# How four stores of a decode-attention backward kernel are cut, and on which queue one row leaves

## The chip, the core and the metric

The kernel runs on one core of one Trainium2 chip. The core has a matrix engine (PE, TensorE), three engines for elementwise work (DVE is VectorE, ACT is ScalarE, POOL is GpSimd), an engine that here only issues transfers (SP, SyncE), and 16 DMA engines that move data between the chip's memory (HBM) and the core's on-chip memory (SBUF). The metric is the device time of one execution in microseconds (us), as a median over runs. The profile is of one execution of its own; its "span" begins and ends inside that execution.

## The reference

Forward attention of a single query row per head over 8192 keys, with 32 heads of width 128 in bfloat16, and its gradients for a given output gradient:

```python
def _fwd_reference(q, k, v):
    scale = q.shape[-1] ** -0.5
    scores = jnp.einsum('bhqd,bhkd->bhqk', q, k) * scale
    attn = _softmax(scores, axis=-1)
    return jnp.einsum('bhqk,bhkd->bhqd', attn, v)

def reference(q, k, v, grad_out):
    ...
    _out, _vjp = jax.vjp(_f, q, k, v)
    _grads = _vjp(grad_out)
    ...
    return (_out0, *[jnp.asarray(_g) for _g in _grads])
```

The inputs are q (1, 32, 1, 128), k and v (1, 32, 8192, 128) and grad_out like q. The kernel is asked for four results: the output O and dQ, which are 32 rows of 128 numbers each (8 KB), and dK and dV, which are as large as k and v (67 MB each). With p the softmax row and ds its gradient, dV is the outer product of p and the head's grad_out row, and dK is the outer product of ds and the head's q row.

## The kernel before, in words

**Tiling.** Two heads make a pair, so there are 16 pairs (`HP`), numbered 0 to 15. The K of a pair is one SBUF tile `Kt` of 128 partitions with 32 KB each, 4 MB (the profile counts it as 4096 KB), and its V is a tile `Vt` of the same size. The tiles are reused in place: when a pair's K has been read for the scores and for dQ, `outer(j, "dk", r)` (L286 to L305) overwrites it with dK, and the tile is stored from there; `Vt` becomes dV in the same way. `outer` does one eighth of a tile at a time (`r` from 0 to 7, one VectorE multiplication at L290 each). There are three K tiles (`K_BUFS`) and two V tiles (`V_BUFS`), so a load into a tile has to wait until the gradient of the pair that used it before has been stored: V of pair 3 goes into the tile from which dV of pair 1 leaves, and K of pair 5 into the tile from which dK of pair 2 leaves.

**Loop.** `for j in range(HP + 1)` (L355) does the softmax part of pair j and the gradient part of pair j-1 (`p_`). For j from 3 to 15, dK of pair j-1 is multiplied out in the middle of the step (r = 0 and 1 at L419 and L420, 2 at L433, 3 at L448, 4 to 7 at L467), then `load_v(j + 1)` is issued; then dV of pair j is multiplied out (L487) and `load_k(j + 2)` issued (L492). For j = 1 and 2 and for the last step, j = 16, the eight dK blocks come in one run (L402 to L407).

**Order.** The order of the instructions on each engine is written out by hand (`tc.manual_schedule()`, L126). All loads and stores of K, V, dK and dV go out on SyncE's queue in the order of the code, except half of dV of pair 0, which GpSimd issues in shares (`share_out`, L116). A transfer that SyncE issues first waits for what it depends on, and everything behind it on SyncE waits too.

**How a store is cut.** `outer` looks up `ENDS` (L18) for its tile: the numbers in it are the block counts after which a piece is stored. `(8,)`, which is what a tile without an entry gets, is one store of 4 MB after the eighth block; `(4, 8)` is two stores of 2 MB, after the fourth and the eighth; `(2, 4, 8)` is 1 MB, 1 MB and 2 MB. The store is issued at L305.

**The end.** In step 16 there is no new pair. dK of pair 15 is multiplied out in eight blocks, and between blocks 5 and 6 (L403) the code puts in `result` (L334 to L341) twice: it turns the collected O and dQ columns into rows through a copy on ACT, a transpose on PE and a second copy on ACT into `fin_sb`, and stores the 32 rows. The third argument says which engine's queue issues that store.

Of the kernel before, what the change touches and what calls it, by code (L numbers as in the profile page):

```python
# [14 lines left out]

XK_BUFS = 3
EARLY = 3
ENDS = {("dv", 1): (4, 8), ("dk", 2): (4, 8), ("dk", 15): (2, 4, 8), ("dv", 15): (4, 8)}  # L18
CH = 16
TB = 4  # L20
R = 4
# [10 lines left out]
def kernel(  # L32
# [11 lines left out]
    nc = tc.nc  # L44
# [44 lines left out]
    def load_v(j):  # L89
        Vt[j] = vpool.tile([P, NT, D], BF16, tag="V", name="Vt")  # L90
        parts = LOADS.get(("v", j), 1)
        for c in range(parts):
            nc.sync.dma_start(slots(Vt[j], c, parts), rows_of(v, j, c, parts))
# [74 lines left out]
    o_all = consts.tile([P, H], F32)  # L168
    dq_all = consts.tile([P, H], F32)
# [99 lines left out]
    def gather_copy(j, which):  # L269
        if j % GP != GP - 1:  # L270
            return
        S = acc["S" + which] = small.tile([P, 4, D], F32, tag="S", name="S_" + which)
        nc.scalar.copy(S[:].rearrange("p j d -> p (j d)"), acc.pop(which)[:])

    def gather(j, which, bank):
        if j % GP != GP - 1:
            return
        S, to = acc.pop("S" + which), (o_all if which == "p" else dq_all)
        pick = lane[:].rearrange("p (w j) -> p j w", j=4)
        at = 8 if which == "p" else 16  # L280
        for i in range(4):
            nc.tensor.matmul(bank[:, at:at + 2 * GP], lhsT=S[:, i, :], rhs=pick[:, i, :],  # L282
                             start=(i == 0), stop=(i == 3), skip_group_check=True)
        nc.scalar.copy(to[:, 2 * (j - GP + 1):2 * j + 2], bank[:, at:at + 2 * GP])

    def outer(j, which, r):  # L286
        x = st[j]
        G, dst = (Kt[j], out_2) if which == "dk" else (Vt[j], out_3)
        rep, row = x["ds"] if which == "dk" else x["p"], qd[j][:, 0 if which == "dk" else 1, :]
        nc.vector.tensor_tensor(  # L290
            slots(G, r, NU).rearrange("p n (a b) -> p n a b", b=R),
            slots(rep, r, NU).unsqueeze(2).to_broadcast([P, CH, D // R, R]),
            row.rearrange("p (a b) -> p a b", b=R).unsqueeze(1).to_broadcast([P, CH, D // R, R]),
            op=ALU.mult)
        if (which, j) == ("dv", 0):
            if (r + 1) * CH == SHARED:
                share_out(rows_of(dst, 0)[:, 0:SHARED, :], G[:, 0:SHARED, :])
            elif r == NU - 1:
                nc.sync.dma_start(rows_of(dst, 0)[:, SHARED:NT, :], G[:, SHARED:NT, :])
            return  # L300
        ends = ENDS.get((which, j), (8,))
        if r + 1 in ends:
            i = ends.index(r + 1)
            a, b = (ends[i - 1] if i else 0) * CH, (r + 1) * CH
            nc.sync.dma_start(rows_of(dst, j)[:, a:b, :], G[:, a:b, :])  # L305
# [25 lines left out]
        nc.vector.tensor_copy(x["ds"][:], ds1[:].unsqueeze(2).to_broadcast([P, NT, R]))  # L331
        window(ds1[:].rearrange("p (g j) -> p g j", j=4))

    def result(src, dst, issuer):  # L334
        half = small.tile([P, H], BF16, tag="half", name="half", bufs=2)
        nc.scalar.copy(half[:], src[:])
        fin_ps = psT.tile([P, 2 * TB, P], BF16, tag="T", name="fin_ps")
        nc.tensor.transpose(fin_ps[0:H, 0, :], half[:], ident[:])
        fin_sb = small.tile([H, D], BF16, tag="fin", name="fin_sb", bufs=2)
        nc.scalar.copy(fin_sb[:], fin_ps[0:H, 0, :])  # L340
        issuer.dma_start(dst.rearrange("b h s d -> (b h s) d"), fin_sb[:])  # L341

    DQ = NG // 4
    NC = NX // TB
# [5 lines left out]
    def half(j, f):  # L350
        for c in range(f * NC, (f + 1) * NC):
            chunk(j, c)
        v_scores(j, f)

    for j in range(HP + 1):  # L355
# [42 lines left out]
        if ends and j > 0:  # L398
            gather_copy(p_, "ds")
            if early:  # L400
                half(j, 0)
            for r in range(NU):  # L402
                if j == HP and r == NU - 2:  # L403
                    result(o_all, out_0, nc.scalar)
                    gather(p_, "ds", st[p_]["m"])
                    result(dq_all, out_1, nc.sync)
                outer(p_, "dk", r)  # L407
            if j + 1 < HP:
                load_v(j + 1)
# [115 lines left out]
```

## Time and profile before

| what | value |
|---|---|
| median of 3 runs | 633.3 us (633.1 to 633.46) |
| the profiled execution's own time | 633.27 us |
| its span | 631.5 us |
| busy in the span: PE, DVE, ACT, POOL | 462.9, 516.2, 205.2, 10.0 us |
| moved by DMA | 268.98 MB, 426 GB/s on average |
| read from and written to HBM | 134.23 MB each |

The profile's page cuts the span into 40 slices of 15.8 us and gives for each the share of time in which the 16 DMA engines were busy, and the rate. The timeline lists the instructions of one engine in order: start, duration, and what it is; "x2" merges two that follow each other. A line with SPq is the moment at which SyncE hands a transfer over, not the transfer. "To landing" is the time from there to the transfer's completion.

### The profile page before, as it was taken

The numbers are of one execution on the slowest core, as the hardware profiler recorded it, in microseconds if no ns is written. First come the engines' busy times: TensorE is split into PE (matmuls) and PEld (weight loads), VectorE is DVE, ScalarE is ACT, GpSimd is POOL, SyncE is SP. The second block draws the span as 40 slices with busy tenths as digits, with TensorE's granted clock in tenths as the row PEclk, the third lists the DMA queues.
The fourth block names the chain that finished last, engine by engine and source line by source line (L and its number), as shares of the span: only waits on it lengthen the run. The fifth ranks groups of instructions, "written<-read, shape, count | busy, mean of one in ns | idle before, by whom it ended". The sixth has DMA issues, their size and how long they took to land.

```text
span 631.5 us, 8017 instructions
## 1 busy us (share of the span) xinstructions
PE 462.9 (73%) x3256; PEld 247.0 (39%) x3256; DVE 516.2 (82%) x654; ACT 205.2 (32%) x460; POOL 10.0 (2%) x21
## 2 busy tenths in 40 slices
PE   4786687778787888676897767957679776796670
PEld 1443354254443525333363432624336243252440
DVE  6589887989889798796978969879597896988873
ACT  2441434053342505234151330603316143160430
POOL 2030000000000000000000000000000000000000
PEclk9989968878698977779877788877897878887785
DMA  8999999999999999999999999999999999999997
GB/s 366 432 400 436 431 435 431 429 422 439 433 431 434 431 431 438 429 432 431 429 432 433 427 432 431 431 432 427 429 436 433 432 431 431 432 431 431 428 420 323
DMA packets 12052, 268.98 MB, mean 426 GB/s; under 512 B 1904, under 2 KB 1904, under 8 KB 1904
## 3 DMA queue, kind: packets, MB, share of 16 engines
q1 hardware_dynamic: 11136, 266.35, 98.4%
q0 software_dynamic: 736, 2.10, 0.8%
q8 instruction: 25, 0.41, 0.2%
q14 instruction: 11, 0.09, 0.0%
q10 hardware_dynamic: 144, 0.02, 0.0%
HBM read 134.23 MB, written 134.23 MB: 425 GB/s over the span
## 4 chain that ended last, share of the span: by engine, by line
DMA 60%; PE 26%; DVE 8%; ACT 3%; issue 1%; DVEq 0%; SPq 0%; ACTq 0%
DMA Vt<-in_v_dram 40%; DMA out_dram<-Vt 19%; PE T_ps L215 15%; PE s_ps L198 4%; PE acc_p L265 4%; DVE Vt L290 2%; ACT XV_sb L220 2%; PE dp_ps L232 2%; DVE Kt L290 2%; DVE XK_sb L188 1%; PE acc_ds L265 1%; DMA Kt<-in_k_dram 1%; DVE sT L205 0%; PE m_ps L282 0%; DVE dpT L243 0%
## 5 line engine op out<-in xcount | busy, mean ns | idle before, releaser
L198 PE MATMUL s_ps<-XK_sb,q_win 128*128 128x512 bf16 x512 | 154.8, 440 | 63.8 <-DVE XK_sb L188 59.1
L290 DVE TENSOR_TENSOR Vt<-p_rep,qd 128x2048 bf16<-128x2048 bf16 x128 | 154.1, 1222 | 40.4 <-PE acc_p L265 30.7
L188 DVE STREAM_TRANSPOSE XK_sb<-Kt 128x1024 f32<-128x1024 f32 x128 | 150.2, 1218 | 37.8 <-DMA Kt<-in_k_dram 34.3
L215 PE MATMUL T_ps<-ident_f,Vt 128*128 128x128 f32 x1024 | 167.5, 317 | 7.0 <-DMA Vt<-in_v_dram 7.0
L220 ACT COPY XV_sb<-T_ps 128x512 f32<-128x512 f32 x256 | 140.0, 589 | 85.6 <-PE T_ps L215 85.1
L290 DVE TENSOR_TENSOR Kt<-ds_rep,qd 128x2048 bf16<-128x2048 bf16 x128 | 149.5, 1214 | 3.1 <-PE acc_ds L265 2.7
L215 PEld LDWEIGHTS T_ps<-ident_f,Vt 128*128 128x128 f32 x1024 | 133.9, 163 | 44.6 <-issue 21.7
L198 PEld LDWEIGHTS <-q_win 128*128 128x128 bf16 x512 | 52.2, 111 | 153.8 <-issue 123.1
L265 PE MATMUL acc_p<-Vt,win 128*32 128x512 bf16 x512 | 55.5, 435 | 3.6 <-ACT win L255 3.6
L440 ACT ACTIVATE e<-sT,nbias 128x128 f32<-128x128 f32 x16 | 8.3, 516 | 147.8 <-DVE nbias L436 147.8
L265 PEld LDWEIGHTS <-win 128*32 128x32 bf16 x1024 | 22.9, 99 | 60.3 <-issue 48.7
L265 PE MATMUL acc_ds<-Kt,win 128*32 128x512 bf16 x512 | 42.5, 427 | 4.6 <-ACT win L255 4.6
L255 ACT COPY win<-ds 64x128 bf16<-64x128 bf16 x32 | 9.5, 296 | 106.5 <-DVE ds L327 106.3
L232 PE MATMUL dp_ps<-XV_sb,do_win 128*32 128x512 bf16 x512 | 34.0, 381 | 13.5 <-ACT XV_sb L220 13.5
L232 PEld LDWEIGHTS <-do_win 128*32 128x32 bf16 x512 | 14.3, 94 | 29.0 <-issue 22.5
L441 PE MATMUL m_ps<-rs,ones_f 128*128 128x1 f32 x32 | 7.5, 305 | 24.4 <-ACT e L440 24.4
L427 PE MATMUL m_ps<-ident_f,top 128*128 128x128 f32 x16 | 4.8, 300 | 23.5 <-DVE top L425 23.5
L205 DVE STREAM_TRANSPOSE sT<-s_ps 128x512 f32<-128x512 f32 x16 | 11.5, 717 | 10.8 <-PE s_ps L198 10.8
L441 PEld LDWEIGHTS m_ps<-rs,ones_f 128*128 128x128 f32 x32 | 6.2, 241 | 27.6 <-ACT e L440 27.6
L452 ACT ACTIVATE p_rep<-e,rinv 128x512 bf16<-128x512 f32 x16 | 11.5, 721 | 13.3 <-DVE rinv L450 13.3
L427 PEld LDWEIGHTS m_ps<-ident_f,top 128*128 128x128 f32 x16 | 2.1, 133 | 31.0 <-issue 25.4
L317 PEld LDWEIGHTS m_ps<-pd,ones_f 128*128 128x128 f32 x32 | 8.8, 286 | 10.1 <-DVE prod L248 9.1
(59 smaller groups left out, 151.5 us busy)
## 6 DMA issues: line engine op xcount, KB each, us to landing
Kt<-in_k_dram SPq DMA_DIRECT2D x14, 4096.0 KB, 29.0
out_dram<-Kt SPq DMA_DIRECT2D x14, 4096.0 KB, 25.0
Vt<-in_v_dram SPq DMA_DIRECT2D x14, 4096.0 KB, 29.0
out_dram<-Vt SPq DMA_DIRECT2D x13, 4096.0 KB, 32.2
out_dram<-Vt SPq DMA_DIRECT2D x5, 2048.0 KB, 17.9
out_dram<-Kt SPq DMA_DIRECT2D x3, 2048.0 KB, 17.8
Kt<-in_k_dram SPq DMA_DIRECT2D x4, 1024.0 KB, 8.0
Vt<-in_v_dram SPq DMA_DIRECT2D x2, 2048.0 KB, 17.4
```

The lines of the kernel that those rows point to most:

```text
L188: nc.vector.transpose(XK[j, u][:].rearrange("p g w i -> p (g w i)"), slots(Kt[j], u, NU).rearrange("p g d -> p (g d)").bitcast(F32))
L198: nc.tensor.matmul(st[j]["s"][:], lhsT=q_win[:, c, at:at + P], rhs=cols[:, c // 2, c % 2], start=(u == 0 and c == 0), stop=(u == NU - 1 an ...
L205: nc.vector.transpose(sT[:].rearrange("p g r -> p (g r)"), x["s"][:])
L215: nc.tensor.transpose(T_ps[:, i, :], words[:, m * P:(m + 1) * P], ident_f[:])
L220: nc.scalar.copy(XV[j][:, b * TB:(b + 1) * TB, :], st[j].pop(("T", c))[:])
L232: nc.tensor.matmul(out[b * QD:(b + 1) * QD, :], lhsT=do_win[:, b // 2, e2, at:at + QD], rhs=cols[:, z, e2, :, b * QD:(b + 1) * QD], start= ...
L255: nc.scalar.copy(win[t * M:(t + 1) * M, :, at:at + 4], src[t * M:(t + 1) * M])
L265: nc.tensor.matmul(acc[which][b * QD:(b + 1) * QD, :], lhsT=win[:, g, at:at + QD], rhs=X[:, 4 * g:4 * g + 4, :].rearrange("p n d -> p (n d)"),
L290: nc.vector.tensor_tensor(slots(G, r, NU).rearrange("p n (a b) -> p n a b", b=R), slots(rep, r, NU).unsqueeze(2).to_broadcast([P, CH, D // ...
L317: nc.tensor.matmul(x["m"][:, 1:3], lhsT=ones_f[:], rhs=x["pd"][:], start=True, stop=True, skip_group_check=True)
L441: nc.tensor.matmul(x["m"][:, 0:1], lhsT=ones_f[:], rhs=rs[:], start=True, stop=True, skip_group_check=True)
L452: nc.scalar.activation(x["p"][:], e[:].unsqueeze(2).to_broadcast([P, NT, R]), ACT.Copy, scale=rinv[:])
```

## The change

Four edits, in two places. dV of pair 1 and dK of pair 2 lose their entries in `ENDS`, so each is stored as one transfer of 4 MB after its eighth block. The last 2 MB of dK of pair 15 are stored as two transfers of 1 MB, after the sixth and the eighth block. `result` loses its third argument: O's rows are issued on SyncE's queue, as dQ's were, and no longer on ACT's.

```diff
-ENDS = {("dv", 1): (4, 8), ("dk", 2): (4, 8), ("dk", 15): (2, 4, 8), ("dv", 15): (4, 8)}
+ENDS = {("dk", 15): (2, 4, 6, 8), ("dv", 15): (4, 8)}
...
-    def result(src, dst, issuer):
+    def result(src, dst):
...
-        issuer.dma_start(dst.rearrange("b h s d -> (b h s) d"), fin_sb[:])
+        nc.sync.dma_start(dst.rearrange("b h s d -> (b h s) d"), fin_sb[:])
...
                 if j == HP and r == NU - 2:
-                    result(o_all, out_0, nc.scalar)
+                    result(o_all, out_0)
                     gather(p_, "ds", st[p_]["m"])
-                    result(dq_all, out_1, nc.sync)
+                    result(dq_all, out_1)
                 outer(p_, "dk", r)
```

The built program has the same instructions in the same order on PE, DVE and POOL; ACT has one fewer (the issue of O's store). On SyncE the pair of half stores becomes one store in two places, and the end reads: dK 15 first quarter, second, third, O's rows, dQ's rows, fourth quarter.

## The prediction

> **What bounds the kernel now.** I read first the page's slices, then its DMA queues.
>
> ```profile
> DMA  8999999999999999999999999999999999999997
> GB/s 366 432 400 436 431 435 431 429 422 439 433 431 434 431 431 438 429 432 431 429 432 433 427 432 431 431 432 427 429 436 433 432 431 431 432 431 431 428 420 323
> ...
> q1 hardware_dynamic: 11136, 266.35, 98.4%
> q8 instruction: 25, 0.41, 0.2%
> ```
>
> The DMA engines are full from the second slice to the last but one; DVE, the busiest compute engine, is at 82%. q1, SyncE's queue, fills 98.4% of the engines' time. So the question of each edit is whether a DMA engine gets more or less to do, or runs dry. The windows answer the second part (the last two columns are the DMA share and GB/s; a share can pass 1, as a packet is counted where it starts):
>
> ```profile
> 60.00:72.00 12.00, 7.78 (x76) 4.74 (x78) 10.57 (x15) 6.76 (x15) 0.00 (x0) 1.00 1.03 443
> 72.00:77.00 5.00, 3.54 (x28) 1.31 (x20) 4.97 (x7) 0.41 (x2) 0.00 (x0) 1.00 1.00 426
> ...
> 129.00:136.00 7.00, 6.57 (x33) 4.82 (x34) 6.86 (x9) 4.06 (x9) 0.00 (x0) 0.55 0.99 426
> ...
> 150.00:600.00 450.00, 341.86 (x2356) 181.18 (x2359) 376.08 (x470) 146.30 (x323) 0.00 (x0) 0.83 1.00 431
> ...
> 620.00:622.00 2.00, 0.00 (x0) 0.00 (x0) 0.65 (x1) 0.00 (x0) 0.00 (x0) 0.50 1.01 419
> 622.00:625.00 3.00, 0.00 (x0) 0.00 (x0) 0.00 (x0) 0.00 (x0) 0.00 (x0) 0.50 1.08 455
> 625.00:628.00 3.00, 0.00 (x0) 0.00 (x0) 0.00 (x0) 0.00 (x0) 0.00 (x0) 0.50 0.80 344
> 628.00:631.40 3.40, 0.00 (x0) 0.00 (x0) 0.00 (x0) 0.00 (x0) 0.00 (x0) 0.50 0.08 34
> ```
>
> The share is about 1 where the edits lie, and falls only from 625 us on, when one engine after the other has finished. For more I took the trace's records of single packets. They don't say on which engine a packet ran, but a packet begins about 4 ns before the recorded end of the one ahead of it, so they can be strung into 16 chains (an inference, which worked out for all 11,136 packets of q1). Three things come out. No chain idles more than 0.6 us in the whole span. A transfer puts 8 packets and a semaphore write on each engine, and takes there, start to start, 9.681 us with 4 MB, 4.863 with 2 MB, 2.453 with 1 MB. And the chains end apart: the first at 626.46, the last four at 628.98, 629.02, 629.57 and 629.82; the span ends 1.7 us after the last. So the end is the load of the fullest DMA engine.
>
> **The change part by part.** What SyncE issues, in its timeline:
>
> ```profile
> 65.15 0.34 SPq L93 DMA_DIRECT2D Vt<-in_v_dram  x1
> 71.66 4.87 SPq L305 DMA_DIRECT2D out_dram<-Vt  x2
> 76.62 0.53 SPq L87 DMA_DIRECT2D Kt<-in_k_dram  x1
> ...
> 113.81 0.34 SPq L87 DMA_DIRECT2D Kt<-in_k_dram  x1
> 129.59 5.46 SPq L305 DMA_DIRECT2D out_dram<-Kt  x2
> 135.15 0.38 SPq L93 DMA_DIRECT2D Vt<-in_v_dram  x1
> ...
> 613.87 2.60 SPq L305 DMA_DIRECT2D out_dram<-Kt  x2
> 618.73 0.34 SPq L341 DMA_DIRECT2D out_dram<-fin_sb  x1
> 620.68 0.34 SPq L305 DMA_DIRECT2D out_dram<-Kt  x1
> ```
>
> *dV 1 whole.* The line at 71.66 holds both halves; the second starts at 71.66 + 4.87 - 0.33 = 76.20. Now all 4 MB leave then, the first half 4.5 us later. Ahead of it in the queue is V 2, issued at 65.15 and landed 19.5 us later (DMA issues), at 84.7: 8.5 us of cover. By chain, V 2 ends between 77.27 and 84.22; a store's first packet came 0.85 us after its issue at the end (620.68, 621.53), so the whole store can begin at 77.05, 0.2 us before the first engine is free. K 3 follows at 76.6 in both kernels, V 3 waits for dV 1 to land, 17.9 us after 76.20, as the second half does now. Nothing behind it moves. Gain: two pieces cost 2 x 4.863 = 9.725 us of each engine, one 9.681: -0.044. With the cover gone the cost is up to 4.5.
>
> *dK 2 whole.* The same. The second half starts at 129.59 + 5.46 - 0.33 = 134.72, 5.1 us after the first. K 4, issued at 113.81, lands 29.0 later at 142.8: 8.1 us of cover; the first chain is through at 136.27, 0.7 us after the store can begin (135.57). -0.044; cover gone, up to 5.1.
>
> *dK 15 in four.* DVE's eight multiplications run from 611.48 for 9.17 us, so the sixth ends at 611.48 + 6/8 x 9.17 = 618.36, and the third quarter leaves there; the fourth at 620.68 as the 2 MB do now. Would the earlier issue let the end come earlier? The second quarter is issued at 613.87 + 2.60 - 0.33 = 616.14 and takes 9.0 to land, until 625.1, so at 620.68 the fullest engine still has 4 us queued: by chain its first packet of the last store is at 624.95. Starting earlier helps engines that are waiting; the only ones that did, for 0.57 and 0.07 us, end at 626.51 and 626.46, over 3 us before the last. Gain 0; cost of one more boundary 2 x 2.453 - 4.863 = +0.043.
>
> *O's rows on SyncE.* ACT loses an issue of 0.33 us at 616.96, in a stretch where its next copy (L284) waits for PE until 617.62: nothing. The rows put two packets of 256 B and a semaphore write on an engine, 0.034 us, on either queue. On SyncE they stand behind the third quarter and ahead of dQ's rows and the last quarter. `fin_sb` of O is ready at 616.93, dQ's at 618.71, so three issues in a row end by 618.36 + 0.33 + 2 x 0.34 = 619.4, or 0.34 after dQ's are ready, 619.1; the last multiplication ends at 620.65. The cover is 1.3 us; without it the fourth quarter leaves later, and that counts on the fullest engine only past 627.4 (624.95 + 2.45). Bounds: 0 and +0.03.
>
> *Semaphores.* A transfer also waits for the one eight places before it, whose semaphore it reuses. In the changed program's waits the fourth quarter inherits dK 14's. That store is issued at 594.56 and lands 16.2 later at 610.8, ten before. In the stretches between, the predecessor is two pairs back. 0.
>
> **Sum**: -0.044 - 0.044 + 0.043 = -0.05 us. The profiled execution has a span of 631.5 and a time of 633.27, so 1.77 lie around it: 631.45 + 1.77 = 633.2. The median, 633.3, is 0.03 above the profiled run. 0.2% of it, 1.27 us, is about what a measurement of this kernel can tell from no change.
>
> **Rivals.** *A, slower: the fullest engine gets more.* Besides the queue's transfers the engines carry instruction fetches (the q8 row: 25 packets of 16 KB; by their records 0.95 us each, 0.87 to 1.07), spread unevenly, and slow packets (median 1.21 us for 32 KB, the longest 1.97). The changed program has one instruction fewer on ACT, and other places for three on SyncE; if that moves a fetch onto the engine that ends last, it costs 0.95 us: 634.2. One stays within 0.2%; from two on (635.1) it is past it. The other way it pays little, since the next engine ends only 0.25 us earlier. Against: PE and DVE, which have most of the instructions, keep every one; the three times before lie within 0.36 us. 17%: 10 for one, 7 for more.
>
> *B, slower: the rings run dry before the whole stores.* For it: the first chain is within 0.2 us of that at 77. Against: only the fullest matters, and it has V 2 until 84.22 and K 4 until 142.36. It decides when the whole store begins after that, some 7 us later than worked out; then it costs up to 4.5 and 5.1, for one of them 637.8. 4%.
>
> *C, faster: the last store is the end.* The span closes with SyncE waiting 9.1 us for the last dK store. If that transfer's size set the end, halving it would give 4.86 - 2.45 = 2.4 us: 630.8; if only the idle seen in front of it counted, 0.57: 632.7. Against: the share of 1.01 and 1.08 from 620 to 625, and the first packets at 624.95. 7%, five of them past 0.2%.
>
> *D, faster: a transfer has a fixed cost that queued work doesn't hide.* One transfer fewer in all. The dearest row for one is the 8 KB of q rows at the start, 3.4 us to landing (DMA issues): 629.8. Against: the steps of 2.45, 4.86 and 9.68 us, nearly in proportion to size. 4%. The Trainium skill, "DMA: Bandwidth & Descriptors", section "Anatomy of one DMA", gives a fixed part of about 2.0 us per transfer beside its bytes, measured on GpSimd's path; by that, exposed, the sum would be -2.0 and the time 631.2. The chains here show 0.043 to 0.044 us for a boundary on SyncE's queue: the rule describes a transfer by itself, and no run here has one in the places edited. The same page, "Rules for kernel authors", wants at least 1 MiB per transfer, and the new quarters are just that; paying 2.0 us at the very end would make 635.2, but the two quarters stored now follow each other without a gap.
>
> **Numbers.** The forecast, no change, has 68%, with a range of its own of 632.7 to 633.8. It holds the band of 0.2% (632.0 to 634.6) but for 1% below and 2% above. Faster: C 5 + D 4 + 1 = 10%. Slower: A 7 + B 4 + 2 = 13%. The rest, 77%, is the same. The range runs from 632.1 to 634.4: it takes in one fetch of A and C's smaller price, and leaves out C's larger (4 or 5), D (4), A's second fetch (7) and B (4), some 19%.
>
> **What will show it.** In the profile after: a DMA share of 0.97 to 1.03 around 77 and 136; dV 1 landing near 94 and dK 2 near 152.5; the third quarter issued near 618.4, O and dQ within 1.3 us behind it, the fourth at 620.7; DMA falling off from 625 and the last packet near 629.8. A share well under 1 around 77 or 136 would speak for B, an end whose slow engine holds one more 16 KB fetch for A, an end more than 1 us earlier for C or D. I am wrong if the fullest engine is not what ends the span.

## The result: 0.19% slower

| | before | changed |
|---|---|---|
| median | 633.1 us (21 runs, 632.46 to 634.49) | 634.35 us (21 runs, 633.26 to 636.27) |
| ratio | | 1.0019, 95% interval 1.0013 to 1.0026 |
| profiled execution, its span | 633.27, 631.5 | 635.82, 634.0 |

The change costs 1.2 us. One run of a version below, the profiled one of the even kernel with whole stores, took 1251.68 us at a granted clock of 0.349 and is in none of the numbers. The changed kernel's shortest run is 0.8 us above the shortest before, its longest 1.8 us above the longest, so the runs also lie further apart. The profiled execution of the changed kernel is one of the longer ones, which makes it useful. Its page first, the slices and the queues:

```profile
DMA  8999999999999999999999999999999999999996
GB/s 366 431 406 435 431 426 431 429 435 431 429 429 430 429 433 435 429 432 427 431 432 433 432 427 431 431 434 429 429 435 427 436 431 432 434 432 429 426 419 267
...
q1 hardware_dynamic: 11040, 266.36, 98.1%
q8 instruction: 25, 0.41, 0.2%
```

The DMA engines together are as full as before in every slice but the last, 267 GB/s where it was 323, and there are as many instruction fetches, 25. The windows of the end say how that slice empties (last columns: granted clock, DMA share, GB/s). First the changed kernel:

```profile
620.00:622.00 2.00, 0.36 (x2) 0.10 (x1) 1.43 (x2) 0.64 (x3) 0.00 (x0) 0.50 1.03 434
622.00:625.00 3.00, 0.00 (x0) 0.00 (x0) 0.00 (x0) 0.00 (x0) 0.00 (x0) 0.50 1.01 420
625.00:628.00 3.00, 0.00 (x0) 0.00 (x0) 0.00 (x0) 0.00 (x0) 0.00 (x0) 0.50 0.90 375
628.00:630.00 2.00, 0.00 (x0) 0.00 (x0) 0.00 (x0) 0.00 (x0) 0.00 (x0) 0.50 0.22 94
630.00:632.00 2.00, 0.00 (x0) 0.00 (x0) 0.00 (x0) 0.00 (x0) 0.00 (x0) 0.50 0.06 25
632.00:634.00 2.00, 0.00 (x0) 0.00 (x0) 0.00 (x0) 0.00 (x0) 0.00 (x0) 0.50 0.02 8
```

and the same stretches of the kernel before:

```profile
628.00:630.00 2.00, 0.00 (x0) 0.00 (x0) 0.00 (x0) 0.00 (x0) 0.00 (x0) 0.50 0.14 57
630.00:632.00 2.00, 0.00 (x0) 0.00 (x0) 0.00 (x0) 0.00 (x0) 0.00 (x0) 0.50 0.00 0
```

A share of 0.06 is one engine of 16. In the changed kernel fifteen engines are done by 630 and a single one works on alone, to 632.7; before, nothing moved after 629.8. So the average load didn't grow; one engine fell behind. The question is which one, and where. SyncE's timeline of the changed kernel:

```profile
39.07 0.35 SPq L299 DMA_DIRECT2D out_dram<-Vt  x1
...
65.31 0.34 SPq L93 DMA_DIRECT2D Vt<-in_v_dram  x1
78.17 0.33 SPq L305 DMA_DIRECT2D out_dram<-Vt  x1
78.59 0.38 SPq L87 DMA_DIRECT2D Kt<-in_k_dram  x1
...
113.97 0.34 SPq L87 DMA_DIRECT2D Kt<-in_k_dram  x1
137.18 0.33 SPq L305 DMA_DIRECT2D out_dram<-Kt  x1
...
614.65 4.87 SPq L305 DMA_DIRECT2D out_dram<-Kt  x3
619.57 2.50 SPq L341 DMA_DIRECT2D out_dram<-fin_sb  x2
622.16 1.16 SPq L305 DMA_DIRECT2D out_dram<-Kt  x1
```

dV 1 leaves at 78.17, 2.0 us later than the 76.20 that I had from the execution before, and dK 2 at 137.18, 2.5 us later than 134.72. Most of the 2 us has nothing to do with the change: the first line, dV 0's second half, which comes before any edited instruction, is at 39.07 here and was at 37.27. The compute that leads up to these stores took about 2 us more in this execution than in the other.

Strung into chains as in the prediction (a chain is one DMA engine's packets, inferred from their times), the packets of the two profiled executions give this (us; "slow chain" is explained below):

```
                                                    before            changed
V 2 ends on the slow chain, the first of the 16     77.27             77.45
dV 1 (second half / whole) issued                   76.20             78.17
the slow chain idle before dV 1                     0                 1.56
V 2 ends on the last of the 16                      84.22             84.54
slow packets on the slow chain, whole span          7.2               8.9
the slow chain ends                                 628.5             632.70
the last of the other chains ends                   629.82            629.95
```

One chain is unlike the others. Nearly every 32 KB packet takes 1.213 us. On this chain, and apart from short bursts on this one alone, many take a little longer (up to 0.13 us each), which adds up to 1.0 to 1.8 us in every 100 us of both traces from 100 us on. (Two chains can be mistaken for each other after packets of theirs end within some ns, so late in the span the identity is followed by this excess. The sums of 7.2 and 8.9 are therefore estimates, the second above all.) In the changed trace the chain that ends at 632.70 shows the excess until 622 us, so the last engine is the slow one. It is also the chain that carries next to nothing of GpSimd's queue: 0.4 us, the others 2.8 to 7.6. That is what `SHARES` does with dV 0: it leaves one engine out. In the kernel before, this engine thus starts some 4.6 us ahead at 77 us, gives that up over 500 us, and ends in the middle of the field. In the changed kernel it sits idle with its queue empty until the first packet of the whole dV 1 comes at 79.01, 0.84 us after the issue, and the head start it lost there is missing at the end.

### The profile page after: what moved, and what is told of

It is laid out like the page before. It is cut to its first block, busy times and chain, and to the rows that moved or that the text cites. A ratio compares the mean times of both kernels' runs of the same rounds, so it can differ in the third digit from the quotient of the medians.

```text
span 634.0 us, 8014 instructions
## 1 busy us (share of the span) xinstructions
PE 466.7 (74%) x3256; PEld 246.8 (39%) x3256; DVE 516.0 (81%) x654; ACT 204.1 (32%) x460; POOL 10.0 (2%) x21
## 4 chain that ended last, share of the span: by engine, by line
DMA 50%; PE 27%; DVE 16%; ACT 3%; issue 2%; DVEq 0%; ACTq 0%; SPq 0%
DMA Vt<-in_v_dram 23%; PE T_ps L215 11%; DMA Kt<-in_k_dram 10%; DMA out_dram<-Vt 9%; DMA out_dram<-Kt 8%; PE s_ps L198 7%; DVE Kt L290 6%; DVE XK_sb L188 4%; PE acc_p L265 3%; DVE Vt L290 2%; ACT XV_sb L220 2%; PE acc_ds L265 2%; PE dp_ps L232 2%; DVE sT L205 1%; PE m_ps L282 1%
## 5 line engine op out<-in xcount | busy, mean ns | idle before, releaser
L198 PE MATMUL s_ps<-XK_sb,q_win 128*128 128x512 bf16 x512 | 156.4, 442 | 66.4 <-DVE XK_sb L188 61.2
L215 PE MATMUL T_ps<-ident_f,Vt 128*128 128x128 f32 x1024 | 165.0, 313 | 5.4 <-DMA Vt<-in_v_dram 5.4
L215 PEld LDWEIGHTS T_ps<-ident_f,Vt 128*128 128x128 f32 x1024 | 130.9, 160 | 43.2 <-issue 20.5
L265 PE MATMUL acc_p<-Vt,win 128*32 128x512 bf16 x512 | 57.0, 449 | 2.9 <-ACT win L255 2.9
L184 ACT COPY do_win<-do_cols 64x4 bf16<-64x4 bf16 x32 | 6.6, 206 | 16.1 <-PE dp_ps L232 15.9
```

The costliest lines, as they stand in the source:

```text
L198: nc.tensor.matmul(st[j]["s"][:], lhsT=q_win[:, c, at:at + P], rhs=cols[:, c // 2, c % 2], start=(u == 0 and c == 0), stop=(u == NU - 1 an ...
L215: nc.tensor.transpose(T_ps[:, i, :], words[:, m * P:(m + 1) * P], ident_f[:])
L265: nc.tensor.matmul(acc[which][b * QD:(b + 1) * QD, :], lhsT=win[:, g, at:at + QD], rhs=X[:, 4 * g:4 * g + 4, :].rearrange("p n d -> p (n d)"),
```

## The experiments

The theory ("the head start"): dV 1 and dK 2, stored whole, come so late that the slow DMA engine, first through V 2 and K 4, runs dry. The rivals: the new order at the end; whole stores costing something in themselves; VectorE's work. All ratios are to the kernel before on the same chip, with a 95% interval. A ratio is not the quotient of the two medians, and differs from it by up to 0.1% (638.47 / 633.39 is 1.0080, the ratio there 1.0071).

**One edit alone, and all but it.**

```diff
 # dV 1 whole alone, on the kernel before
-ENDS = {("dv", 1): (4, 8), ("dk", 2): (4, 8), ("dk", 15): (2, 4, 8), ("dv", 15): (4, 8)}
+ENDS = {("dk", 2): (4, 8), ("dk", 15): (2, 4, 8), ("dv", 15): (4, 8)}
 # all but dV 1, on the changed kernel
-ENDS = {("dk", 15): (2, 4, 6, 8), ("dv", 15): (4, 8)}
+ENDS = {("dv", 1): (4, 8), ("dk", 15): (2, 4, 6, 8), ("dv", 15): (4, 8)}
```

> The kernel before with one of the four edits: dV of pair 1 stored whole. Theory (the head start): one of the 16 DMA engines moves its packets slower than the others all through the span and gets almost nothing of pair 0's shares, so it is the first to finish V 2, at 77.3 to 77.5 us. The whole store of dV 1 comes at 76.2 to 78.2, depending on the execution, and that engine runs dry for up to some 3 us, which it cannot make up; it ends last. Expected: the whole loss of the change, 634.3 (ratio 1.0015 to 1.0025), and an idle stretch on one chain near 77. Rival (the end): the order of the last five issues on SyncE is what costs; then 633.1, ratio 1.000. Rival (dK 2): 633.1 too.

> The changed kernel with dV of pair 1 back in two halves; the other three edits stay. The head start: 633.1, ratio 0.9995 to 1.0005, no chain idle over 0.6 us near 77. The rivals (the end, or dK 2): the loss stays, 634.3, ratio 1.0015 to 1.0025.

dV 1 whole alone: 634.09 against 633.39, ratio 1.0015 (1.0005 to 1.0025); 632.96 to 636.24 over 12 runs. As expected in size; but the profiled execution was a short one (dV 1 out at 75.94, no idle stretch, 633.39), so this trace doesn't show the loss. All but dV 1: 634.38, ratio 1.0020 (1.0009 to 1.0031). This was a miss: I had put the whole loss on dV 1, and the other three edits cost as much by themselves. The two don't add to 0.35%, as independent costs would. What the runs of the second kernel do show is a strong tie to the clock that TensorE was granted: 636.7 at 0.827, 633.02 at 0.852, correlation -0.93 over 11 runs. For the changed kernel it is -0.70 (21 runs), for the kernel before on that chip 0.05 (29 runs). It is no rule, though: for dV 1 whole alone it is -0.12 (12 runs, the longest, 636.24, at 0.843), and for the kernel before on the chip of the last experiments -0.43 (27 runs). So I widened the theory to dK 2: both are the same mechanism, and a head start can be lost only once. In the changed trace, where it went at 77 us, dK 2 could begin at 137.18 + 0.84 = 138.02 and the slow chain had K 4 until 139.37.

The trace of that second kernel does not bear the theory out. Its profiled run, 634.38 like its median, issued dK 2 at 134.58, so that it could begin at 135.42, and the slow chain had K 4 until 136.76. No chain ran dry there or at 77, the slow chain ended at 629.33, and the last packet, at 630.95, was on an engine without the small excess. A time of 634.38 is within the range of the kernel before on that chip (632.12 to 634.74), so this one execution refutes nothing, but it supports nothing either.

**dK 2 alone, the end alone.**

```diff
 # dK 2 whole alone, on the kernel before
+ENDS = {("dv", 1): (4, 8), ("dk", 15): (2, 4, 8), ("dv", 15): (4, 8)}
 # the end alone, on the changed kernel
+ENDS = {("dv", 1): (4, 8), ("dk", 2): (4, 8), ("dk", 15): (2, 4, 6, 8), ("dv", 15): (4, 8)}
```

> The kernel before with dK of pair 2 stored whole and nothing else. The head start, widened to two places: the slow DMA engine is also the first to finish K 4 (136.8 us in the run without dV 1 whole), and the whole store of dK 2 comes between 134.6 and 137.2 by the clock that TensorE is granted up to there, so in executions of low clock the engine runs dry. Expected: nearly the loss of the changed kernel with dV 1 in halves, 634.0 to 634.5 (ratio 1.001 to 1.002), times from 633 to 636.7, and a time that falls as the granted clock of the run rises (correlation below -0.6). The end as the cause: 633.3, ratio 1.000, no correlation.

> The changed kernel with both pairs of halves put back, so that only the end differs from the kernel before: dK 15 in four quarters, O's rows on SyncE. The head start: 633.2 to 633.5, ratio 0.9995 to 1.0005, spread like before (within some 2.5 us). The end as the cause: 634.0 to 634.5, ratio 1.001 to 1.002.

The end alone: 633.36 against 633.41, ratio 1.0000 (0.9992 to 1.0009). The four quarters and O on SyncE cost nothing. dK 2 alone: 633.29, ratio 1.0003 (0.9992 to 1.0013), 632.24 to 635.6, correlation with the clock -0.58 (12 runs; before on that chip -0.22, 23 runs). Two of its runs (634.71 and 635.6, at clocks of 0.836 and 0.833) are longer than any of the kernel before there (634.47), so there may be a tail, but the median is not moved. That misses what I expected (1.001 to 1.002). By itself this leaves dK 2 open; the next pairs show that it can run dry.

**The suspected wait made longer.** An eighth can be multiplied out again without changing its result, since the multiplication does not read what it overwrites. Two repeats put the store 2.3 us later (`store=False` returns from `outer` behind the multiplication).

```diff
 # dV 1 (dK 2 in the same way at L467), once with this tile stored whole, once in halves; the other in halves
+            if j == 1 and r == NU - 1:
+                for _ in range(2):
+                    outer(j, "dv", r, store=False)
             outer(j, "dv", r)
```

> dV of pair 1 whole, and the last eighth of dV 1 multiplied out three times over, so that the store comes two multiplications (2 x 1.15 = 2.3 us) later. The head start: the dry stretch grows by 2.3 us and the time with it, to 636.0 to 636.8 (ratio 1.0045 to 1.006). If whole stores cost something in themselves (longer packets), or the cost lies elsewhere: as with dV 1 whole alone, 634.3, or as before, 633.1.

> The control: the kernel before with the same two extra multiplications, dV 1 in halves. The second half comes 2.3 us later behind a first half of 4.9 us, so nothing runs dry. The head start: 633.1 to 633.4, ratio 1.000 to 1.0005. If VectorE's extra 2.3 us are what costs in the late kernel, the same 2 to 3 us show here.

> dK of pair 2 whole, and its last eighth multiplied out three times over, so that the store comes 2.3 us later still (the other tiles are stored as before). The head start: dK 2 whole has 1 to 1.5 us of cover left on the slow engine in a quick execution (K 4 ends there at 136.3 to 136.9, the store can begin at 135.4); 2.3 us more uses that up in every execution, not only in those of low clock. Expected 634.3 to 635.8 (ratio 1.0015 to 1.004), most of it in the runs of lowest clock. If dK 2 whole is harmless and what showed with dV 1 in halves was something else: 633.3, ratio 1.000.

> The control: the same two extra multiplications with dK 2 in halves. The head start: 633.2 to 633.5, ratio 0.9995 to 1.0007. If VectorE's extra 2.3 us in pair 3's step are what costs, the same as with dK 2 whole.

| | whole, late | halves, late |
|---|---|---|
| dV 1 | 638.47 (5 runs), ratio 1.0071 (1.0059 to 1.0083) | 633.61 (11 runs), ratio 0.9997 (0.9988 to 1.0005) |
| dK 2 | 636.88 (5 runs), ratio 1.0054 (1.0041 to 1.0067) | 633.48 (11 runs), ratio 0.9996 (0.9987 to 1.0005) |

VectorE's extra work is free here; a whole store that comes late, with no half ahead of it, is not. So the engines run dry before dK 2 too, once its store comes 2.3 us later. Both losses came out larger than I had said (636.0 to 636.8, and 634.3 to 635.8). SyncE's timelines, dV 1 whole and late, then dV 1 in halves and late, then dK 2 whole and late:

```profile
80.38 0.33 SPq L307 DMA_DIRECT2D out_dram<-Vt  x1
```

```profile
71.31 7.39 SPq L307 DMA_DIRECT2D out_dram<-Vt  x2
```

```profile
138.89 0.33 SPq L307 DMA_DIRECT2D out_dram<-Kt  x1
```

The whole dV 1 leaves at 80.38, a second half in the control at 71.31 + 7.39 - 0.33 = 78.37. By chain, V 2 was over on the slow one at 76.93; it idled 4.4 us, and three others 0.4 to 1.9. With dK 2 late, seven chains idled until 139.73 to 139.84, the longest for 3.45 us. The two medians lie 5.1 and 3.6 us above the kernel before, near those stretches. In both, the first packet came 0.84 us after the issue.

**No head start to lose.** The shares are replaced by one plain transfer, eight rows for each engine.

```diff
-                share_out(rows_of(dst, 0)[:, 0:SHARED, :], G[:, 0:SHARED, :])
+                nc.gpsimd.dma_start(rows_of(dst, 0)[:, 0:SHARED, :], G[:, 0:SHARED, :], max_dma_last_dim=8192)
```

> The kernel before with the first half of dV 0 issued by GpSimd as one transfer, eight rows to each DMA engine instead of the shares (this takes the slow engine's head start away: it gets 16 packets of 0.31 us more, 4.9 us), and dV 1 and dK 2 whole. The head start: the slow engine ends last in any case, 633.4 + 4 to 5 us, and since it no longer comes first at 77 and 137, storing whole costs nothing: the same time as its partner with halves, within 0.05% of each other. If whole stores cost by themselves (longer packets, later landing), 1.2 us more than the partner.

> The partner: the same even first half of dV 0, with dV 1 and dK 2 in halves as before. The head start: 637 to 639, the slow engine ending last by several us, and the same as its partner with whole stores. Otherwise: 1.2 us less than the partner. Should no engine be slow, the even split would cost nothing: 633.4.

Whole 637.45 (5 runs), ratio 1.0068 (1.0055 to 1.0081); halves 637.79 (6 runs), ratio 1.0067 (1.0053 to 1.0080). Without the head start, storing whole costs nothing that these intervals show. That speaks against a price of whole stores as such; one below the width of the intervals, or one paid by engines that have time left at the end, would not show. And the even split costs 4.4 us, near the 4.9 us of packets that the slow engine gets. Windows of the even kernel with halves:

```profile
628.00:630.00 2.00, 0.00 (x0) 0.00 (x0) 0.00 (x0) 0.00 (x0) 0.00 (x0) 0.50 0.76 324
630.00:632.00 2.00, 0.00 (x0) 0.00 (x0) 0.00 (x0) 0.00 (x0) 0.00 (x0) 0.50 0.10 41
632.00:634.00 2.00, 0.00 (x0) 0.00 (x0) 0.00 (x0) 0.00 (x0) 0.00 (x0) 0.50 0.08 33
```

The rate falls to that of one or two engines at 630 and stays there for over three us, the same picture as in the changed kernel.

**Both whole; and a cut that sends something earlier.**

```diff
 # both whole, the end as before
+ENDS = {("dk", 15): (2, 4, 8), ("dv", 15): (4, 8)}
 # cut at six, the rest as in the changed kernel
+ENDS = {("dv", 1): (6, 8), ("dk", 2): (6, 8), ("dk", 15): (2, 4, 6, 8), ("dv", 15): (4, 8)}
```

> dV 1 and dK 2 whole, the end as before. The head start: the whole loss of the change, 634.2 to 634.8 (ratio 1.0012 to 1.0025); the two don't add up, because what the slow engine loses at 77 it no longer has to lose at 137. If the loss needs the changed end too: 633.4 to 633.8.

> The changed kernel with dV 1 and dK 2 cut after the sixth eighth: 3 MB leave two multiplications (2.3 us) earlier than the whole store, 1 MB after the eighth. The head start: a dry stretch is 0 to some 3 us long, so this removes nearly all of it: 633.2 to 633.7, ratio 0.9998 to 1.0008. If the number of stores or the size of the rows is what counts, and not the moment at which the first piece leaves, it depends on neither and the loss might stay: 634.3.

Both whole: 633.94 against 633.31 (634.2 to 634.8 expected), ratio 1.0018 (1.0006 to 1.0030), the whole loss with the old end. In its profiled execution dV 1 went out at 76.38, the slow chain idled 0.30 us, and it was the last to end, at 630.47. Cut at six: 633.28, ratio 1.0000 (0.9991 to 1.0009). SyncE's timeline of that kernel:

```profile
73.86 2.60 SPq L305 DMA_DIRECT2D out_dram<-Vt  x2
76.56 0.72 SPq L87 DMA_DIRECT2D Kt<-in_k_dram  x1
...
132.35 2.60 SPq L305 DMA_DIRECT2D out_dram<-Kt  x2
135.05 0.38 SPq L93 DMA_DIRECT2D Vt<-in_v_dram  x1
```

and its end:

```profile
628.00:630.00 2.00, 0.00 (x0) 0.00 (x0) 0.00 (x0) 0.00 (x0) 0.00 (x0) 0.50 0.19 78
630.00:632.00 2.00, 0.00 (x0) 0.00 (x0) 0.00 (x0) 0.00 (x0) 0.00 (x0) 0.50 0.00 0
```

With 3 MB issued at 73.86 and 132.35, and their first packets possible 0.84 us later, there are 2.2 and 2.8 us left before the slow chain is through V 2 (76.87) and K 4 (135.97). No engine is left working alone at the end. The version keeps the new end and is as fast as the kernel before; none of the versions beats it.

## Why the prediction was wrong

**The step that failed** is the cover of dV 1 and dK 2, and with it rival B. The prediction had the right place and even the right row: "the whole store can begin at 77.05, 0.2 us before the first engine is free". Two readings of it were wrong.

The first: "only the fullest matters, and it has V 2 until 84.22 and K 4 until 142.36. It decides when the whole store begins after that, some 7 us later than worked out". I took the engine that is first at 77 us for one with little to do. It is the slow one, which `SHARES` sends ahead; its early place is load that it still has to make up. The chains showed this: 7 us apart at 84, only 3.4 us apart at the end, so somebody gives up a head start on the way. Its packets were there to be added up by chain, and I added up only idle time. The point from which it decides is therefore the first engine, not the last: 0.2 us for dV 1, 0.7 for dK 2. dV 1 alone at 1.0015, the late pairs, and the even pair show it. The prediction said "Nothing behind it moves"; the runs showed a loss of 1.2 us, and the profiled one an engine that idled 1.56 us at 77.45 and ended last, at 632.70.

The second: a margin of 0.2 us was read from one execution. The issue moved by 2.0 us in the next. A cover is worth what it is in a late execution. With halves there were 4.5 and 5.1 us more of it, which the cut at six shows to be more than is needed.

The sign that the prediction had set for B could not show this. It was a DMA share well under 1 around 77. Here is the stretch in the kernel before, in which no engine idled there, and then in the changed one:

```profile
77.00:79.00 2.00, 0.38 (x2) 0.30 (x2) 1.34 (x8) 0.28 (x1) 0.00 (x0) 0.88 0.93 401
```

```profile
77.00:79.00 2.00, 2.00 (x17) 0.86 (x10) 1.97 (x5) 0.41 (x2) 0.00 (x0) 1.00 1.02 442
```

The share is the mean of 16 engines and counts a packet where it starts; one idle engine is lost in it.

**The sum** of -0.044 twice was moreover too fine to see: no experiment here resolves it, with intervals of 0.1% or wider.

**Luck.** The median of 634.35 lies inside the range of 632.1 to 634.4, by 0.05 us. That edge was there for one more instruction fetch (rival A, 634.2), which is not what happened, and B's price stood outside it. The narrow range of the forecast itself, 632.7 to 633.8, missed.

**Right:** the end. The bounds were +0.04 to +0.07 us for the extra quarter and O on SyncE; the end alone measured 1.0000 (0.9992 to 1.0009). In the changed execution the cover of 1.3 us was in fact used up (dQ's rows were out at 619.57 + 2.50 = 622.07, the last multiplication had ended at 621.43, and the fourth quarter was issued at 622.16), and still it cost nothing, because the engine that ends last came to that quarter only at 630.24, as the second, wider margin had it.

**The other rivals.** A: the number of instruction fetches is the same, and the engine that ends last in the changed trace is late from slow packets and a dry queue, not from fetches. C and D gave the wrong sign. That the DMA engine which finishes last sets the end held in every trace that was strung into chains: the span ends 1.2 to 1.7 us after the last packet. I had the wrong engine for it.

**Open.** The profiled loss exceeds the dry stretch: 1.56 us idle, 4.2 later at the end of the slow chain. Its packets were also slower in that execution (8.9 against 7.2 us of small excess, and a few long packets), which may be chance. The same trace has another dry stretch: before dK 14's store, issued at 596.80 (594.56 before), two other chains idled about 0.6 us each until 597.7. Whether the granted clock delays the stores, through PE's work before 77 and 137 us, was not tried; the correlations are with the mean clock of a run, and not all versions show one. Why the other three edits cost 1.0020 on one chip, when their parts cost 1.0003 (dK 2) and 1.0000 (the end) on another, was not settled either. The intervals overlap, and the one trace of the three edits together shows no dry stretch. So the loss of the whole change is traced to the late whole stores; how it divides between dV 1 and dK 2 is not shown.

## What to carry to other kernels

Where transfers fill all DMA engines, ask for each engine on its own when its queue empties and whether it is early because it has little to do or because it was sent ahead; a queue that is long enough on the last engine says nothing about the first. Read a margin against the spread of the executions, not from one: a store whose first piece leaves a few us early costs 0.04 us of DMA time and insured here against a loss of 1.2 us in the median and some 3 us in the longest runs. Two edits that spend the same reserve need not add up (1.0015 and 1.0020 apart, 1.0019 together), so taking one back need not show what it costs.

## What the runs showed of the hardware

- One DMA engine of the 16 moved its packets slower than the rest over the whole span: about 7 to 9 us more in 631, packets of 32 KB at up to 0.13 us over the usual 1.213. Even shares of dV 0 in place of `SHARES` cost 4.4 us of 633.
- A boundary between two stores on one queue cost an engine 0.043 to 0.044 us when work stood behind it; a store issued into an empty queue brought its first packet after 0.84 us.
- A store that stands ahead of every edit (dV 0's second half) came at 37.27 in one execution and at 39.07 in another. Spreads of this size go unseen where a half store has left 4.5 us earlier, and show where the cover is 0.2 us.
